# Reordering the pass over x in an induced-attention kernel: transposes, induced products, first chunk's scores and one projection

## The chip, the cores and the metric

One core of a Trainium2 chip runs the whole kernel. The metric is device time in microseconds (us) of one execution, lower is better; a kernel's figure is the median of several runs. Beside the runs there is one profiled execution, from whose trace every row below is taken. Engines: PE is the matmul engine (PEld its weight loads), DVE the vector engine, ACT the scalar engine, POOL the GpSimd engine, SP the engine that only issues DMAs here. A name such as SPq or ACTq is the engine's issuing side.

## What is computed

`x` has 12480 tokens of 128 features, `inducing` 32 rows of 128. Two attentions, then two MLPs of inner width 2048, all in float32 (the weights arrive as float64 and are narrowed on the chip):

```python
def mab(q, kv):
    s = scale * (q @ kv.transpose(0, 2, 1))
    s = s - s.max(-1, keepdims=True)
    a = np.exp(s)
    a /= a.sum(-1, keepdims=True) + 1e-09
    return a @ kv
h = mab(I, x)            # 32 inducing rows over all of x
y = mab(x, h)            # every token over the 32 rows of h
g = (y @ w_in1);  y1 = (g * np.cos(g)) @ w_out1
u = (y1 @ w_in2); y2 = (u / (1 + np.exp(-u))) @ w_out2
```

## The kernel before, in words

**Order.** Each engine runs its instructions in the order in which the program writes them (a manual schedule). Where an instruction waits, everything behind it on that engine waits too, and so it is on SP's queue of DMAs.

**Pass over x (the prologue).** The 98 token tiles are loaded in 8 heads, `heads = [(0, 8), (88, 10), (8, 16), (24, 16), (40, 16), (56, 16), (72, 11), (83, 5)]` (first tile, count), each in two halves, all from SP (L328, L330). Between heads 2 to 5 and their successors SP also issues four 512 KB pieces of the float64 weights (`fetch`, L133). Before the data come, PE does `SPIN` warm-up matmuls on zeros (L343). For each head k: PE transposes its tiles into PSUM (`transposes`, L392), ACT copies them out (`untile`, L402), PE forms the scores against the inducing rows (`scores`, L419), DVE takes their maximum (`maximum`, L432), PE and DVE fold it over the four groups (`row_max`, `bias`, `bound`, L442 to L469), ACT takes the exponentials and a rescaling factor (`exps`, L484, L498), DVE transposes them and adds up the denominators (`turn`, L507, L514), PE multiplies them with x (`induced`, L539), and DVE rescales the running sum (`rescale`, L552). In the loop over i, `induced` and `rescale` run two heads behind; the last three heads follow after the loop. In the same stretch POOL and DVE narrow the first weight pieces (`narrow_body` L142, `narrow_tail` L149, `narrow_sign` L154, `narrow_join` L157 and L165).

**Hand-over.** One matmul gives h transposed (L638), DVE copies it to `hT4` (L646). The first MLP's input weights are projected through h (`project`, L653, four pieces of 512 columns; `project_hi` on ACT, L662, and `project_lo` on DVE, L665, make them into `hw[0..3]`), since y @ w_in1 is a @ (h @ w_in1). ACT squares all of the narrowed w_in1 (`win`, L640) for a bound that selects one of two cosine forms (`flag`).

**Second attention.** Tokens go in chunks: 8 tiles, five of 16, 10 tiles. For a chunk PE forms scores (`weigh_scores`, L211), DVE transposes them, then come maximum, subtraction, exponential, sum, division, transposing back and a split in a high and a low part (`weigh_take` to `weigh_split`, L233 to L255). The first chunk does all of it in the prologue. Attention weights then go into `stk[:, b % 2, :]`, the right-hand side of the first MLP's matmuls for block b. For block 0 (tiles 0 to 3) this is done by eight small matmuls and a copy on ACT (L697, L704); for every other block by `spread` (L296), DMAs from SP: one per group of tokens and per quarter of the stack. Block 1 (tiles 4 to 7) has four groups, so 16 DMAs of 16 KB; a block of a 16-tile chunk has one group, so 4 DMAs.

**Main loop.** A step s handles unit u = s of the first MLP: eight units to a block. `mlp1_in` (L761) is the first thing that PE does in a step, then the down products of an earlier unit (`mlp1_out`, L853, L843); ACT takes the cosine (L796), DVE multiplies (L800). Unit u's `mlp1_in` writes one of two PSUM buffers, so it waits until DVE has multiplied unit u-2. Narrowing of further weights is spread over the steps by tables (`bodied`, `tailed`, `signed`, `joined`); `narrow_sign` and `narrow_join` share one buffer, `sign`, that POOL reads last. From step 11 on the second MLP runs beside the first.

## Time and profile before

| | us |
|---|---|
| median of 3 runs (lowest to highest) | 967.62 (966.91 to 967.96) |
| the profiled execution | 967.38 |
| its span in the trace | 965.2 |

The span runs from the first to the last instruction recorded; 2.2 us of the execution lie outside it. In the rows, a line gives a start in us from the span's beginning, a duration in us, the engine and line, operation, out<-in by names, the shapes and a count, and in square brackets the idle time before it with what ended it.

### The profile page before, as it was taken

The page shows a single profiled execution, that of the slowest core. Times are in us where ns is not written, and L with a number is a line of the kernel's source. Part 1 is how long each engine was busy: PE and PEld are TensorE (multiplying, and loading weights), DVE is VectorE, ACT ScalarE, POOL GpSimd, SP SyncE. Part 2 cuts the span into 40 slices and gives each one's busy share as a digit, 9 for nine tenths or more (in the row PEclk, how much of TensorE's full clock was granted, in tenths as well). Part 3 has the DMA queues.
Part 4 walks back from the last instruction along what each step waited for, and adds up shares of the span by engine and source line. Part 5 has one row for each costly group of instructions (what it writes and reads, how often), then busy time and mean ns, then how long its engine had stood idle before and what let it go on. Part 6 is the DMA issues. An engine that isn't in the chain of part 4 may idle for free.

```text
span 965.2 us, 11951 instructions
## 1 busy us (share of the span) xinstructions
PE 951.8 (99%) x4480; PEld 758.0 (79%) x4481; DVE 779.3 (81%) x784; ACT 691.6 (72%) x725; POOL 517.2 (54%) x274
## 2 busy tenths in 40 slices
PE   8899999999999999999999999999999999999997
PEld 5456778888878888878888887888887888888896
DVE  4889888988887988888988887988888888878751
ACT  5687768777668776767777777777767777677774
POOL 3346545654545655554655544655455554555565
PEclk9999999999999999999999999999999999999999
DMA  9341000001010010010010010010010100100001
GB/s 356 112 138 45 6 18 11 14 20 22 2 22 12 12 22 12 12 22 12 12 22 12 12 22 12 12 22 7 17 22 1 22 14 9 21 12 5 13 11 20
DMA packets 65484, 28.19 MB, mean 29 GB/s; under 512 B 54440, under 2 KB 60040, under 8 KB 65416
## 3 DMA queue, kind: packets, MB, share of 16 engines
q1 hardware_dynamic: 64760, 27.24, 10.8%
q8 instruction: 37, 0.61, 0.3%
q14 instruction: 31, 0.25, 0.1%
q10 hardware_dynamic: 656, 0.09, 0.1%
HBM read 14.79 MB, written 6.39 MB: 22 GB/s over the span
## 4 chain that ended last, share of the span: by engine, by line
PE 95%; DMA 2%; DVE 1%; issue 0%; SPq 0%; ACT 0%; POOL 0%; ACTq 0%; POOLq 0%; DVEq 0%
PE acc L843 53%; PE h L896 28%; PE h L761 9%; PE acc L853 4%; DMA x_sb<-in_x_dram 2%; PE s L211 1%; PE pt L392 0%; PE hp L539 0%; SPq L328 0%; PE s L419 0%; DVE et L507 0%; DVE c L800 0%; DVE mx L432 0%; POOL lo L925 0%; PE misc L455 0%
## 5 line engine op out<-in xcount | busy, mean ns | idle before, releaser
L920 POOL TENSOR_TENSOR lo<-s,hi 128x1024 fp32r<-128x1024 f32 (+3 forms) x189 | 446.7, 2364 | 381.0 <-ACT hi L919 359.6
L843 PE MATMUL acc<-hi,wo 128*128 128x512 f32 (+3 forms) x1520 | 406.8, 389 | 0.0
L843 PEld LDWEIGHTS acc<-hi,wo 128*128 128x128 f32 x1520 | 282.5, 188 | 61.5 <-issue 3.7
L800 DVE TENSOR_TENSOR h<-h,c 128x1024 f32<-128x1024 f32 (+3 forms) x188 | 226.1, 1203 | 123.9 <-ACT c L796 123.7
L796 ACT ACTIVATE c<-h,half_pi 128x1024 f32<-128x1024 f32 (+3 forms) x200 | 219.2, 1096 | 146.9 <-PE h L761 146.1
L911 ACT ACTIVATE s<-h 128x1024 f32<-128x1024 f32 (+3 forms) x200 | 201.2, 1006 | 76.6 <-PE h L896 71.8
L896 PE MATMUL h<-yhi,wi 128*128 128x512 f32 (+3 forms) x800 | 244.2, 386 | 0.0
L843 PE MATMUL acc<-lo,wo 128*128 128x512 f32 (+3 forms) x760 | 232.6, 387 | 0.1
L807 DVE CAST hi<-h 128x1024 fp32r<-128x1024 f32 (+3 forms) x188 | 224.9, 1196 | 6.5
L833 DVE TENSOR_TENSOR lo<-h,hi 128x1024 fp32r<-128x1024 f32 (+3 forms) x188 | 223.9, 1191 | 5.7
L919 ACT CAST hi<-s 128x1024 fp32r<-128x1024 f32 (+3 forms) x189 | 195.3, 1033 | 6.1
L896 PEld LDWEIGHTS h<-yhi,wi 128*128 128x128 f32 x800 | 148.8, 188 | 30.7 <-issue 0.5
L843 PEld LDWEIGHTS acc<-lo,wo 128*128 128x128 f32 x760 | 141.9, 188 | 31.2 <-POOL lo L925 0.4
L896 PE MATMUL h<-ylo,wi 128*128 128x512 f32 (+3 forms) x400 | 154.3, 386 | 0.0
L761 PE MATMUL h<-stk,hw 128*128 128x512 f32 (+3 forms) x400 | 126.0, 396 | 1.4 <-ACT stk L704 0.7
L761 PEld LDWEIGHTS h<-stk,hw 128*128 128x128 f32 x400 | 74.1, 188 | 26.8 <-issue 6.5
L896 PEld LDWEIGHTS h<-ylo,wi 128*128 128x128 f32 x400 | 75.1, 188 | 15.2
L877 ACT CAST yhi<-acc 128x512 fp32r<-128x512 f32 (+3 forms) x25 | 14.4, 576 | 15.1 <-PE acc L843 15.0
L943 DVE STREAM_TRANSPOSE o<-acc 128x512 f32<-128x512 f32 (+3 forms) x25 | 17.3, 694 | 9.3 <-PE acc L843 9.3
L853 PE MATMUL acc<-c,wf 128*128 128x512 f32 x48 | 22.5, 591 | 0.0
L878 DVE TENSOR_TENSOR ylo<-acc,yhi 128x512 fp32r<-128x512 f32 (+3 forms) x25 | 16.7, 669 | 5.4 <-ACT yhi L877 5.3
L800 DVE TENSOR_TENSOR c<-h,c 128x1024 f32<-128x1024 f32 x12 | 14.6, 1216 | 2.4 <-ACT c L796 1.9
(133 smaller groups left out, 320.6 us busy)
## 6 DMA issues: line engine op xcount, KB each, us to landing
out_dram<-o SPq DMA_DIRECT2D x80, 64.0 KB, 1.9
x_sb<-in_x_dram SPq DMA_DIRECT2D x8, 512.0 KB, 9.2
raw<-in_moe_w_in_dram SPq DMA_DIRECT2D x8, 512.0 KB, 6.5
raw<-in_moe_w_out_dram SPq DMA_DIRECT2D x8, 512.0 KB, 4.5
stk<-ahi SPq DMA_DIRECT2D x40, 64.0 KB, 2.0
stk<-at SPq DMA_DIRECT2D x40, 64.0 KB, 2.0
x_sb<-in_x_dram SPq DMA_DIRECT2D x3, 256.0 KB, 3.7
x_sb<-in_x_dram SPq DMA_DIRECT2D x2, 320.0 KB
```

What stands on the lines that cost most here:

```text
L761: nc.tensor.matmul(ps[:, a, 0:n], lhsT=hw[f // 4][:, f % 4 * P : (f % 4 + 1) * P], rhs=stacks[b][:, 0:n], start=True, stop=True,)
L796: nc.scalar.activation(cs, h, AF.Sin, bias=half_pi, scale=1.0)
L800: nc.vector.tensor_tensor(cs if whole else h, h, cs, ALU.mult)
L807: nc.vector.tensor_copy(hi[:, :, 0:n], h)
L833: nc.vector.tensor_tensor(lo[:, :, 0:n], h, hi[:, :, 0:n].bitcast(F32), ALU.subtract)
L843: nc.tensor.matmul(acc[:, 0:n], lhsT=wt[:, 2 * j + a, :], rhs=gt[:, a, 0:n], start=(j == 0 and p == 0 and a == 0), stop=(j == NJ - 1 and p ...
L853: nc.tensor.matmul(acc[:, 0:n], lhsT=w[:, 2 * j + a, :], rhs=c[:, a, 0:n], start=(j == 0 and a == 0), stop=(j == NJ - 1 and a == 1),)
L896: nc.tensor.matmul(ps[:, a, 0:n], lhsT=wt[:, fs], rhs=yt[:, 0:n], start=(p == 0), stop=(p == 2),)
L911: nc.scalar.activation(sv, hid2.pop(u)[:, :, 0:n], AF.Silu)
L919: nc.scalar.copy(hv, sv)
L920: nc.gpsimd.tensor_tensor(lv, sv, hv.bitcast(F32), ALU.subtract)
L943: nc.vector.transpose(o.rearrange("p t d -> p (t d)")[:, 0:n], acc2.pop(b)[:, 0:n])
```

## The change

- `SPIN` goes from 8 to 5, and the weight pieces are fetched after heads 3 to 6 instead of 2 to 5.
- `transposes(1, 0)` moves ahead of `scores(0)`. Head 0's transposed tiles lie tile by tile in `xF`, so ACT's copy is straight and `scores(0)` reads them with a stride.
- The loop does the induced products of heads 0 to 3 at i = 2, 3, 5, 6; those of heads 4 to 7 follow after the loop.
- Adding up the denominators moves from DVE (in `turn`) to POOL (`add_up`, after `exps`), and so does the small multiplication `foldz`.
- The narrowing of weight pieces 4 and 5 is scaled one place earlier and later in the program; the sign of piece 4 is taken just before `hT4` is written; the join of piece 5 goes from step 0 to step 1 of the main loop.
- The last piece of w_in1 lies in the buffer `s2`, `win` is a quarter shorter, and the squares are taken in two instructions.
- The first chunk's scores are formed token by token (the tile is the stationary operand, `hT4` the moving one), in two halves of four tiles. The first half is brought to the end in the prologue. The second half's maximum, subtraction and exponential are done there too; its division, transposing and split are left to steps 2, 4 and 5, and its 16 DMAs into `stk[:, 1, :]` are issued at the end of step 5.
- DVE instead of ACT copies block 0's stack; projection 3 with its two finishing instructions goes to step 1.

```diff
-    SPIN = 8
+    SPIN = 5
...
-            if 2 <= k < 2 + RAW:
+            if 3 <= k < 3 + RAW:
                 fetch()
...
+    rest = {
+        "span": (MT, FIRST - MT),
+        "s2": sft["at"][:, MT * Q : 2 * MT * Q].rearrange("p (t m) -> p t m", m=M),
+        "sm": sft["sm"][:, 0:MT, :],
+        "at": sft["at"][:, 0 : MT * Q],
+        "hi": sft["hi"][:, 0 : MT * Q],
+        "lo": sft["at"][:, 0 : MT * Q],
+    }
...
-    chunk_soft = [weigh_view(*span) for span in chunks]
+    chunk_soft = [rest] + [weigh_view(*span) for span in chunks[1:]]
...
+            if k == 0:
+                for g in range(G):
+                    nc.tensor.matmul(
+                        ps[g * Q : (g + 1) * Q, 0:WF],
+                        lhsT=indT,
+                        rhs=xF[:, :, g * Q : (g + 1) * Q],
...
+        def add_up(k):
             if k == 0:
-                nc.vector.tensor_copy(zacc[0], zk[:, 0:1])
+                nc.gpsimd.tensor_copy(zacc[0], zk[:, 0:1])
             else:
...
+                nc.gpsimd.tensor_scalar(
+                    zacc[k % 2],
+                    zacc[(k - 1) % 2],
+                    al[:, k : k + 1],
+                    zk[:, k : k + 1],
+                    ALU.mult,
+                    ALU.add,
+                )
...
+        transposes(1, 0)
         scores(0)
         maximum(0)
-        transposes(1, 0)
+        behind = {2: 0, 3: 1, 5: 2, 6: 3}
...
-            if 0 <= k < NP:
+            add_up(i - 1)
+            if 0 <= k <= NP:
                 narrow_body(k, True)
                 narrow_tail(k, True)
-            if i >= 2:
-                induced(i - 2)
+            if i in behind:
+                induced(behind[i])
...
+        h4, h5, h6, h7 = range(end - 3, end + 1)
         untile(end, 0)
         transposes(end, 1)
+        row_max(end - 1)
         untile(end, 1)
-        row_max(end - 1)
+        induced(h4, (0, KT // 2))
         scores(end)
...
+        induced(h4, (KT // 2, KT))
         row_max(end)
+        hps[h5] = other()
+        induced(h5, (0, KT // 2))
         turn(end - 1)
         bias(end)
         bound(end)
         exps(end)
...
+        add_up(end)
+        induced(h5, (KT // 2, KT))
+        rescale(h4)
+        induced(h6)
+        rescale(h5)
         turn(end)
-        narrow_sign(NP)
...
-        nc.vector.tensor_scalar_mul(foldz, fold, rz)
-        rescale(end)
+        nc.gpsimd.tensor_scalar(foldz, fold, rz, 1.0, ALU.mult, ALU.mult)
+        rescale(h7)
...
+        narrow_sign(NP)
         nc.vector.tensor_copy(hT4, misc[:C, None, 0:M].to_broadcast([C, G, M]))
...
+        half = [ps_s.tile([P, W], F32, tag="s1", name="s2") for _ in range(2)]
+        for t in range(FIRST):
+            nc.tensor.matmul(
+                half[t // MT][:, t % MT * M : (t % MT + 1) * M],
+                lhsT=xF[:, t, :],
+                rhs=hT4[:, 0, :],
...
+        for ps, e in zip(half, (eA[:, :, 0:M], eB)):
+            v = ps[:, 0 : MT * M].rearrange("p (t m) -> p t m", m=M)
+            nc.vector.tensor_reduce(out=mA, in_=v, axis=AX.X, op=ALU.max)
+            nc.vector.tensor_tensor(e, v, mA.to_broadcast(wide), ALU.subtract)
+            nc.scalar.activation(e, e, AF.Exp, scale=scale)
+        project(0)
...
+        nc.vector.tensor_reduce(out=mA, in_=eA, axis=AX.X, op=ALU.add)
+        nc.vector.reciprocal(mA, mA)
+        nc.vector.tensor_tensor(nA, eA[:, :, 0:M], mA.to_broadcast(wide), ALU.mult)
+        nc.vector.transpose(atA, flat(nA))
+        nc.scalar.copy(hiA, atA)
...
+        nc.vector.tensor_tensor(loA, atA, hiA.bitcast(F32), ALU.subtract)
         nc.scalar.activation(warm, ones, AF.Silu)
...
+        project_lo(hw[0], halves(0))
...
-        nc.scalar.copy(stk[:, 0, :], top)
+        project(2)
+        nc.vector.tensor_copy(stk[:, 0, :], top)
         stacks[0] = stk[:, 0, :]
-        spread(1, first | {"lo": lo0.bitcast(F32)})
...
+        for i in (1, 2):
+            project_hi(hw[i], halves(i))
+            project_lo(hw[i], halves(i))
...
-    joined = {5: 0, 6: 2, 7: 4, 8: 6, 9: 8, 10: 10, 11: 12, 12: 13, 13: 14, 14: 15, 15: 16}
+    joined = {5: 1, 6: 2, 7: 4, 8: 6, 9: 8, 10: 10, 11: 12, 12: 13, 13: 14, 14: 15, 15: 16}
...
+    rest_plan = {2: "norm", 4: "turn", 5: "split"}
...
-            for b in range(2, NB):
-                if s == b * NJ - (2 if b == 2 else 5 if blocks[b][0] == 1 else FILL):
+            for b in range(1, NB):
+                if s == b * NJ - (3 if b == 1 else 2 if b == 2 else 5 if blocks[b][0] == 1 else FILL):
                     spread(b, chunk_soft[blocks[b][0]])
...
             if s == 1:
-                soften(chunk_soft[1], "scores")
+                two = psh.tile([P, 2, 512], F32, tag="h2", name="s2")
+                nc.tensor.matmul(
+                    two[:, 0, :],
+                    lhsT=hT4.rearrange("c g m -> c (g m)"),
+                    rhs=flat(sft["s2"]),
...
+                weigh_scores(chunk_soft[1], two[:, 1, :])
...
+            if s == 1:
+                project_hi(hw[3], two[:, 0, :])
+                project_lo(hw[3], two[:, 0, :])
```

## Rows read from the trace of the kernel before

**Rows 1.** Busy us of each engine, share and instructions.

```profile
PE 951.8 (99%) x4480; PEld 758.0 (79%) x4481; DVE 779.3 (81%) x784; ACT 691.6 (72%) x725; POOL 517.2 (54%) x274
```

**Rows 2.** Busy time by stretch (count), then granted clock, DMA share, GB/s.

```profile
50.00:60.00 10.00, 10.00 (x29) 5.20 (x28) 9.04 (x13) 7.62 (x11) 3.59 (x4) 1.00 0.42 134
```

**Rows 3.** Timeline of the first 38 us: warm-up, transposes, products.

```profile
1.19 3.60 PE L343 MATMUL spin<-idle 128*128 128x512 bf16 x8 [1.19 <-DVE ones L351]
4.96 1.53 PE L392 MATMUL pt<-ident,x_sb 128*128 128x128 f32 x8
7.21 0.64 PE L419 MATMUL s<-xF,indT 128*32 128x256 f32 x8 [0.73 <-ACT xF L402]
21.05 1.06 PE L392 MATMUL pt<-ident,x_sb 128*128 128x128 f32 x8 [0.59 <-DMA x_sb<-in_x_dram]
22.13 1.06 PE L539 MATMUL hp<-x_sb,et 128*32 128x128 f32 x32
35.22 0.85 PE L539 MATMUL hp<-x_sb,et 128*32 128x128 f32 x22 [0.84 <-DVE hacc L552]
37.83 0.29 DVE L646 COPY hT<-misc 128x128 f32<-128x128 f32 x1 [0.50 <-PE misc L638]
```

**Rows 4.** Timeline from the first chunk's scores to the first unit.

```profile
39.90 0.52 DVE L238 TENSOR_TENSOR s<-s,m 128x256 f32<-128x256 f32 x1
43.58 0.62 PE L697 MATMUL st<-lo,pick 128*128 128x128 f32 x4
43.86 2.70 DVE L665 SCALAR_TENSOR_TENSOR hw<-hw,s_w,hwps 128x512 fp32r<-128x512 f32 x4
44.93 1.21 PE L761 MATMUL h<-stk,hw 128*128 128x512 f32 x4 [0.73 <-ACT stk L704]
```

**Rows 5.** DVE's timeline, units 0 to 2.

```profile
47.03 1.23 DVE L800 TENSOR_TENSOR c<-h,c 128x1024 f32<-128x1024 f32 x1 [0.48 <-issue]
48.18 0.42 DVE L154 TENSOR_SCALAR sign<-raw 128x512 int32<-128x512 int32 x1
48.63 0.69 DVE L157 SCALAR_TENSOR_TENSOR sign<-body,sign 128x512 int32<-128x512 int32 x1
49.24 1.22 DVE L800 TENSOR_TENSOR c<-h,c 128x1024 f32<-128x1024 f32 x1
50.77 0.43 DVE L154 TENSOR_SCALAR sign<-raw 128x512 int32<-128x512 int32 x1 [0.32 <-POOL wf L165]
51.12 1.22 DVE L800 TENSOR_TENSOR c<-h,c 128x1024 f32<-128x1024 f32 x1
```

**Rows 6.** Timeline of POOL's join and of the first MLP's units 2 and 8.

```profile
48.31 0.73 PE L761 MATMUL h<-stk,hw 128*128 128x512 f32 x2 [0.64 <-DVE c L800]
49.47 1.27 POOL L165 TENSOR_TENSOR wf<-sign,tail 128x512 int32<-128x512 int32 x1 [9.33 <-DVE sign L157]
61.09 1.02 PE L761 MATMUL h<-stk,hw 128*128 128x512 f32 x2
```

**Rows 7.** SP's timeline: block 1's spread, first and last of sixteen.

```profile
43.06 1.25 SPq L296 DMA_DIRECT2D stk<-ahi  x2
...
52.70 1.22 SPq L296 DMA_DIRECT2D stk<-lo  x2
```

**Rows 8.** Issuing time of these DMAs (ns, min/median/max); landing after issue.

```profile
L296 SPq DMA_DIRECT2D stk<-lo x8: 529/588/591, 44.4 to 53.3; - x8
DMA to landing us min/median/max: 1.7/1.8/3.3
```

**Rows 9.** Busy time by stretch at the kernel's end.

```profile
958.00:959.00 1.00, 0.48 (x2) 0.19 (x1) 0.35 (x1) 0.00 (x0) 0.16 (x1) 1.00 0.03 8
961.00:962.00 1.00, 0.00 (x0) 0.00 (x0) 0.00 (x0) 0.00 (x0) 0.00 (x0) 0.82 0.49 91
962.00:963.00 1.00, 0.00 (x0) 0.00 (x0) 0.00 (x0) 0.00 (x0) 0.00 (x0) 0.50 0.10 25
```

**Rows 10.** The chain of waits, the warm-up pair after the pass over x.

```profile
37.79 0.43 PE spin L343 x2
```

More of the change, by code (lines that the diff above doesn't have):

```diff
@@ L172, in narrowed @@
         if name == "in1":
-            return win[:, j * PC : (j + 1) * PC]
+            return flat(sft["s2"]) if j == NP - 1 else win[:, j * PC : (j + 1) * PC]
         if name in whole_of:
@@ L255, in weigh_split, with project_hi, project_lo @@
         lo_on.tensor_tensor(st["at"], st["at"], st["hi"].bitcast(F32), ALU.subtract)
+    rest = {
[6 more added lines that the diff above has]
+    }
+    def project_hi(h, ps):
+        nc.scalar.copy(h, ps)
+    def project_lo(h, ps):
+        nc.vector.scalar_tensor_tensor(
+            out=h,
+            in0=h.bitcast(F32),
+            scalar=s_w,
+            in1=ps,
+            op0=ALU.mult,
+            op1=ALU.add,
+        )
     blocks, first_of = [], []
@@ L602, in tile_induced_attention_then_two_mlps @@
         exps(end - 1)
-        narrow_body(NP, True)
-        narrow_tail(NP, True)
-        induced(end - 2, (0, KT // 2))
+        add_up(end - 1)
+        narrow_body(NP + 1, True)
+        narrow_tail(NP + 1, True)
+        induced(h4, (KT // 2, KT))
         row_max(end)
-        induced(end - 2, (KT // 2, KT))
+        hps[h5] = other()
+        induced(h5, (0, KT // 2))
         turn(end - 1)
@@ L626, in tile_induced_attention_then_two_mlps @@
         )
-        induced(end)
-        rescale(end - 1)
+        hps[h7] = other()
+        induced(h7)
+        rescale(h6)
         spin = ps_h.tile([P, SW], F32, tag="hp", name="spin")
@@ L659, in project @@
             )
-        def project_hi(i):
-            nc.scalar.copy(hw[i], hwps[i // 2][:, i % 2, :])
-        def project_lo(i):
-            nc.vector.scalar_tensor_tensor(
-                out=hw[i],
-                in0=hw[i].bitcast(F32),
-                scalar=s_w,
-                in1=hwps[i // 2][:, i % 2, :],
-                op0=ALU.mult,
-                op1=ALU.add,
-            )
-        first = chunk_soft[0]
-        weigh_scores(first, ps_s.tile([P, W], F32, tag="s1", name="s2")[:, 0:WF])
@@ L676, in tile_induced_attention_then_two_mlps @@
-        for i in range(3):
-            project(i)
-        sums = misc[0:1, 128 : 128 + M + 1]
-        nc.tensor.matmul(sums, lhsT=ones, rhs=sq, start=True, stop=True)
-        project(3)
-        weigh_take(first)
-        weigh_centre(first, nc.vector)
-        weigh_exp(first)
-        project_hi(0)
-        nc.scalar.activation(warm, ones, AF.Silu)
-        weigh_norm(first, nc.vector)
-        weigh_turn(first)
-        for i in range(1, 4):
-            project_hi(i)
-        hi0, at0 = first["hi"], first["at"]
@@ new lines, in tile_induced_attention_then_two_mlps @@
+        wide = [P, MT, M]
+        eB = rest["s2"]
+        for ps, e in zip(half, (eA[:, :, 0:M], eB)):
[4 more added lines that the diff above has]
+        project(0)
+        sums = misc[0:1, 128 : 128 + M + 1]
+        nc.tensor.matmul(sums, lhsT=ones, rhs=sq[:, 0 : M + 1], start=True, stop=False)
@@ new lines, in tile_induced_attention_then_two_mlps @@
+        nc.tensor.matmul(
+            sums[:, M : M + 1], lhsT=ones, rhs=sq[:, M + 1 : M + 2], start=False, stop=True
+        )
+        project(1)
+        project_hi(hw[0], halves(0))
+        nc.vector.tensor_reduce(out=mA, in_=eA, axis=AX.X, op=ALU.add)
[3 more added lines that the diff above has]
+        nc.scalar.copy(hiA, atA)
+        most = pw.tile([1, 2], F32, tag="top", name="most")
@@ L694, in tile_induced_attention_then_two_mlps @@
+        nc.vector.tensor_reduce(out=most[:, 0:1], in_=sums[:, 0:M], axis=AX.X, op=ALU.max)
+        nc.vector.tensor_tensor(most[:, 1:2], most[:, 0:1], sums[:, M : M + 1], ALU.mult)
+        nc.vector.tensor_scalar(flag, most[:, 1:2], 1.5**2, None, ALU.is_gt)
+        nc.vector.tensor_tensor(loA, atA, hiA.bitcast(F32), ALU.subtract)
+        nc.scalar.activation(warm, ones, AF.Silu)
+        project_lo(hw[0], halves(0))
         top = ps_s.tile([P, W], F32, tag="s1", name="st")
-        for i, v in enumerate((hi0, lo0)):
+        for i, v in enumerate((hiA, loA)):
@@ L992, in chunk_step @@
         def chunk_step(k, s):
+            if k == 0:
+                return rest_plan.get(s)
             if k == 1:
@@ L997, in attend @@
         def attend(s, early):
-            for k in range(1, NK):
+            for k in range(NK):
                 for at in (s, s + 0.25, s + 0.5):
```

83 lines of the change are left out of this document (45 added, 38 removed).

## The prediction

> **What bounds the kernel now.** I read the page first, for the engines' shares: PE is busy for 951.8 of 965.2 us [rows 1]. Then the busy time by stretch, to see where that share comes from: PE fills its stretch completely from 50 us on while the granted clock is 1.00 [rows 2], and it goes on so to its last matmuls [rows 9]. So a change that touches the first 50 us and eight steps after them can act in two ways only: unit 2's matmuls, from which PE has no more gaps (48.31 us, [rows 6]), move; or a gap opens later in PE, which nothing can win back. I therefore read the timeline of the first 62 us engine by engine, carry each edit forward to the start of unit 8 (61.09 us, [rows 6]), and put its shift on the end. The sum is made against the profiled execution, 967.38 us, 0.24 below the median of the three runs.
>
> **First transposes.** Three warm-up matmuls fewer are 3 x 3.60/8 = 1.35 us [rows 3]. They were over just before the first transposes, which showed no wait for their data, so the gain is between 0 (the tiles land no sooner) and 1.35; I take 0.4. Head 1's transposes fill the 0.73 us in which PE waited for ACT before the first scores [rows 3]; taken as 0.6. The strided reading of `xF` I cost at nothing: the same columns pass through PE. Together -1.0 us. Against it: the first eight warm-ups run at 0.45 us each, the pair after the pass at 0.215 [rows 3, 10], so PE begins at the lower of its two clock levels (1.2 of 2.4 GHz), whatever the stretch's 1.00 says. With less work ahead of the transposes it may stay there longer; at 0 to 1.5 us, I put it at 0 and keep the rest for the range.
>
> **The loop.** PE waited 0.59 us for head 5's tiles [rows 3]; now one 512 KB piece fewer stands ahead of them on SP's queue, and the wait goes. A head's induced products take up to 1.06 us of PE [rows 3]; they leave the loop at i = 4 and come back behind it. There PE has waits to put them in (0.84 us ahead of one group alone, [rows 3]). I take -1.2 us for the loop and +0.1 for the stretch behind it; bounds -0.6 (the wait alone) and -1.8. The denominators' sums on POOL are small beside its scalings and only the last one is near the path. The sign of piece 4 now fills DVE's 0.50 us of idle time before `hT4` [rows 3] and leaves the path of the last heads; with `foldz` now passing through POOL I count the two as equal.
>
> **From hT4 to the first unit.** Before: hT4 ends at 37.83 + 0.29 = 38.12, unit 0 starts at 44.93, 6.81 us [rows 3, 4]. After, with DVE's price for 128x128 between the 0.29 of the copy and the 0.52 of a subtraction twice as wide [rows 3, 4], 0.32 taken: eight passes of 128-wide weights on PE, 8 x 0.13 [rows 3], 1.05; maximum and subtraction of both halves, 4 x 0.32; sum, reciprocal, product and transposing back, 1.15; three small flag operations, which cover ACT's copy, 0.5; low part 0.33; `project_lo` of piece 0, 2.70/4 = 0.68 [rows 4], which covers the four low matmuls (0.62, [rows 4]); DVE's copy of the stack 0.75, which with projection 2 on PE is 0.3 more than it was on ACT; gaps 0.1. That is 6.1, so -0.7 us. Bounds -1.2 and 0. The prologue thus gives -1.0 - 1.2 + 0.1 - 0.7 = **-2.8 us** at unit 2.
>
> **Steps 1 to 5: DVE.** From here I count from DVE's first product (47.03 us before, [rows 5]). Products, signs and joins follow each other at 1.15, 0.45 and 0.61 us from start to start [rows 5]. Before, the third product began at 51.12 - 47.03 = 4.1. Now step 1 has join 5 and directly behind it sign 6, which must wait until POOL has read `sign`: 0.84 us from the join's start to POOL's, and POOL's 1.27 [rows 5, 6]. Product 1 starts at 1.6, the join at 2.75, POOL ends at 4.85, sign 6 starts at 4.9, then comes the new `project_lo` of piece 3 (0.68), and product 2 starts at 5.9, 1.8 later than before. Unit 4 waits for its buffer; PE's pitch is (61.09 - 48.31)/6 = 2.13 us [rows 6], so it cannot catch up. Step 2 adds the second half's sum, increment and reciprocal on DVE, about 0.8 us: another 0.35 at unit 5. PE would be ready for unit 8 at 16.2 instead of 61.09 - 47.03 = 14.1: **+2.2 us** if nothing else held it. Bounds 0 (cosines or PE were later anyway) and 2.6.
>
> **Step 8: the spread.** Before, SP issued block 1's sixteen DMAs from 43.06 to 53.92 [rows 7], over 7 us ahead of unit 8, so they cost nothing. Now they come behind step 5. DVE transposes the second half in step 4, at 12.3 to 12.6 by the count above; ACT's high part is ready at 12.9, POOL's low part, behind join 7, at 14.2. Two DMAs go at once, fourteen after that. One takes SP 0.529 to 0.588 us [rows 8], and the last two of sixteen started 9.64 us after the first two [rows 7]; at 0.63 from start to start the last starts at 14.3 + 13 x 0.63 = 22.5 and lands 1.8 later [rows 8], at 24.3. `mlp1_in` of unit 8 is PE's first work in step 8 and reads the whole stack, so unit 8 and everything behind it on PE waits from 16.2 to 24.4: 8.1 us. Unit 8 thus moves from 14.1 to 24.4, **+10.3 us** including the 2.2 above. Without DVE's delay it is +8.1. While PE stands, DVE, ACT and POOL finish step 7 and can go no further.
>
> The Trainium skill's page "DMA: Bandwidth & Descriptors", section "Issuing engines are not separate DMA queues", says that the time which a sequencer takes to initiate a DMA "is usually small relative to the DMA itself". The trace disagrees here, 0.59 us against 1.8 from issue to landing [rows 8]; by the rule the spread would be in place about 2 us after the low part, at 16.3, and the time would be that of the hidden spread below.
>
> **The clock after the gap.** At the kernel's end PE's last matmuls are at 958.5; the granted clock falls at about 961.6 and is 0.50 from 962 on [rows 9]. A gap of 8.1 us is longer than that, so I expect the lower level when unit 8 starts. At the kernel's start the warm-ups stayed there for all of their 3.60 us [rows 3, 10]; as much again would lose half of it, **+1.7 us**. Bounds 0 and 3.
>
> **Sum.** 967.38 - 2.8 + 10.3 + 1.7 = 976.6 us.
>
> **Rivals.** *Cheaper gap* (chance 0.2): the wait is there, but the clock stays up (974.9), or DVE's delay is hidden and the clock stays up (967.38 - 2.8 + 8.1 = 972.7). For it: the lower level never shows in the middle of this trace; against it, there is no comparable gap. *No gain ahead* (0.12): the pass over x does not get shorter, because loads set its pace or PE's clock rises later; then 976.6 + 2.1 = 978.7. For it speaks the wait for x [rows 3]. *Hidden spread* (0.1): the transfers are in place when unit 8 comes. Then 967.38 - 2.8 + 2.2 = 966.8, or 964.6 if DVE's delay is hidden too: faster or the same. It needs 14.3 + 13d + 1.8 - 14.1 - 2.8 below 0, an issue pitch d under 0.06 us; the lowest in the trace is 0.529 [rows 8]. *Forecast* (0.58): 976.6.
>
> **How the numbers follow.** I forecast the likeliest, 976.6. The range takes in the cheaper gap and the missing gain, and leaves out the hidden spread and the far ends: 971.8 (972.7 with 0.9 more won in the prologue) to 979.6 (978.7 with 0.9 more lost to the clock). A difference of under 0.2%, 1.9 us, cannot be told from none here. Slower holds all cases but the hidden spread, 0.9; of that, same 0.04 and faster 0.06, since an error in the reading of the queue would bring the gain of the prologue with it.
>
> **What would show it.** Unit 0 at about 42.1 us and DVE's first product near 44.2; DVE idle for some 1.4 us behind join 5, waiting for POOL; sixteen DMAs of 16 KB on SP from about 57 to 67 us; PE idle some 8 us at the first matmul of unit 8, released by a DMA into `stk`; a stretch with granted clock below 1.00 behind it. A spread issued before step 4, a pitch far under 0.5 us, or PE without a gap between 55 and 70 us would make the prediction wrong.

## The result, and the profile after

| | before | after |
|---|---|---|
| median (lowest to highest), us | 967.54 (966.91 to 967.96) | 980.22 (979.06 to 981.21) |
| runs | 4 | 4 |
| the profiled execution, us | 967.38 | 980.07 |
| its span, us | 965.2 | 978.3 |

The changed kernel takes 1.013 times as long, 95% interval 1.0117 to 1.0143: 12.7 us slower. That is the forecast's sign, and 0.6 us above the upper end of its range.

I read the rows of after in the order of the prediction's steps: up to unit 2, unit 2 to unit 8, behind unit 8. First PE's timeline up to unit 2 (to be set beside [rows 3, 4, 6]).

```profile
1.19 2.32 PE L365 MATMUL spin<-idle 128*128 128x512 bf16 x5 [1.19 <-DVE ones L373]
...
3.68 1.97 PE L421 MATMUL pt<-ident,x_sb 128*128 128x128 f32 x8
6.66 0.74 PE L421 MATMUL pt<-ident,x_sb 128*128 128x128 f32 x5 [1.01 <-DMA x_sb<-in_x_dram]
7.33 0.64 PE L447 MATMUL s<-xF,indT 128*32 128x256 f32 x8
...
9.84 0.71 PE L462 MATMUL s<-xT,indT 128*32 128x320 f32 x8
...
29.27 0.78 PE L462 MATMUL s<-xT,indT 128*32 128x352 f32 x8
...
31.15 0.27 PE L484 MATMUL misc<-ident,mx 128*1 128x128 f32 x1 [0.74 <-DVE mx L474]
...
36.02 0.38 PE L675 MATMUL misc<-zacc,fold 128*128 128x1 f32 x2 [0.69 <-POOL zacc L558]
...
37.56 0.38 PE L694 MATMUL misc<-foldz,hacc 128*128 128x32 f32 x2
...
43.41 0.66 PE L761 MATMUL st<-hiA,pick 128*128 128x128 f32 x4 [0.87 <-ACT hiA L750]
...
45.39 1.17 PE L823 MATMUL h<-stk,hw 128*128 128x512 f32 x4
...
49.03 0.72 PE L823 MATMUL h<-stk,hw 128*128 128x512 f32 x2 [0.62 <-DVE c L862]
```

The same marks in the kernel before: the scores of head 1 (`128x320`, ten tiles), those of head 6 (`128x352`, eleven tiles), and the product that ends the pass.

```profile
10.44 0.71 PE L419 MATMUL s<-xT,indT 128*32 128x320 f32 x8
...
30.53 0.78 PE L419 MATMUL s<-xT,indT 128*32 128x352 f32 x8
...
37.38 0.41 PE L638 MATMUL misc<-foldz,hacc 128*128 128x32 f32 x2
```

Unit 0 starts at 45.39 us instead of 44.93, unit 2 at 49.03 instead of 48.31. Where the forecast has 2.8 us won, 0.7 are lost. The first transposes start 1.28 us earlier, but head 1's, now in front of the scores, wait 1.01 us for their data. Head 1's scores still come 0.60 us sooner than before and head 6's 1.26 sooner; behind these the lead is lost, and the pass ends 0.18 us later.

Then PE around unit 8, and SP's queue in the same stretch (to be set beside [rows 6, 7]).

```profile
61.50 0.98 PE L823 MATMUL h<-stk,hw 128*128 128x512 f32 x2
62.32 1.88 PE L915 MATMUL acc<-c,wf 128*128 128x512 f32 x4
72.32 1.19 PE L823 MATMUL h<-stk,hw 128*128 128x512 f32 x2 [8.12 <-DMA stk<-at]
73.31 3.62 PE L915 MATMUL acc<-c,wf 128*128 128x512 f32 x4
75.94 1.72 PE L823 MATMUL h<-stk,hw 128*128 128x512 f32 x2
```

```profile
60.70 1.25 SPq L318 DMA_DIRECT2D stk<-ahi  x2
...
69.58 1.22 SPq L318 DMA_DIRECT2D stk<-at  x2
```

PE stands for 8.12 us, and what ends it is a DMA into the stack: the sixteen were issued from 60.70 to 70.80 us. From unit 2 to unit 8 it takes 72.32 - 49.03 = 23.29 us, before 61.09 - 48.31 = 12.78 [rows 6]: +10.51. The first four `acc` matmuls behind the gap take 3.62 us instead of the 1.88 ahead of it. The busy time by stretch tells why; columns: the stretch, its length, busy us (and instructions) of PE, PEld, DVE, ACT and POOL, then the granted clock, DMA share and GB/s.

```profile
64.00:66.00 2.00, 0.20 (x1) 0.00 (x0) 1.76 (x3) 0.27 (x2) 1.26 (x1) 1.00 0.11 26
66.00:68.00 2.00, 0.00 (x0) 0.00 (x0) 0.36 (x1) 0.55 (x1) 1.26 (x1) 0.78 0.10 25
68.00:70.00 2.00, 0.00 (x0) 0.00 (x0) 0.00 (x0) 0.00 (x0) 0.00 (x0) 0.50 0.10 25
...
74.00:76.00 2.00, 2.00 (x5) 0.81 (x3) 1.30 (x2) 1.22 (x2) 0.00 (x0) 0.50 0.79 313
76.00:78.00 2.00, 2.00 (x6) 1.11 (x5) 0.52 (x1) 0.31 (x1) 1.28 (x1) 0.66 0.00 0
78.00:80.00 2.00, 2.00 (x7) 1.06 (x6) 1.16 (x2) 1.97 (x4) 0.00 (x0) 1.00 0.00 0
```

PE's last matmul ahead of the gap ends at 64.20; the clock goes to 0.50 (1.2 GHz) in the stretch from 66 to 68 and is at 1.00 (2.4 GHz) again from 78. DVE, ACT and POOL do nothing from 68 to 72. From unit 8 to the end of the span it takes 978.3 - 72.32 = 905.98 us, before 965.2 - 61.09 = 904.11: +1.87. So the span's +13.1 us are 0.72 + 10.51 + 1.87; the execution is 12.7 us longer, since 0.4 us less of it lie outside the span.

DVE's timeline of units 0 to 2 shows the wait that the prediction had behind join 5 (to be set beside [rows 5]).

```profile
50.41 0.68 DVE L157 SCALAR_TENSOR_TENSOR sign<-body,sign 128x512 int32<-128x512 int32 x1
52.55 0.43 DVE L154 TENSOR_SCALAR sign<-raw 128x512 int32<-128x512 int32 x1 [1.46 <-POOL wf L165]
52.89 0.74 DVE L271 SCALAR_TENSOR_TENSOR hw<-hw,s_w,s 128x512 fp32r<-128x512 f32 x1
53.55 1.22 DVE L862 TENSOR_TENSOR c<-h,c 128x1024 f32<-128x1024 f32 x1
```

### The profile page after: what moved, and what is told of

It is laid out like the page before. It is cut to its first block, busy times and chain, and to the rows that moved or that the text cites. A ratio compares the mean times of both kernels' runs of the same rounds, so it can differ in the third digit from the quotient of the medians.

```text
span 978.3 us, 11983 instructions
## 1 busy us (share of the span) xinstructions
PE 955.7 (98%) x4488; PEld 760.3 (78%) x4488; DVE 778.4 (80%) x779; ACT 692.3 (71%) x729; POOL 521.4 (53%) x286
## 3 DMA queue, kind: packets, MB, share of 16 engines
HBM read 14.79 MB, written 6.39 MB: 22 GB/s over the span
## 4 chain that ended last, share of the span: by engine, by line
PE 94%; POOL 1%; DVE 1%; SPq 1%; ACT 1%; issue 1%; DMA 1%; ACTq 0%; POOLq 0%; DVEq 0%
PE acc L905 52%; PE h L958 27%; PE h L823 9%; PE acc L915 3%; SPq L318 1%; PE pt L421 1%; DMA x_sb<-in_x_dram 0%; PE s L211 0%; POOL wf L165 0%; DVE sign L157 0%; PE hwps L711 0%; ACT e L526 0%; POOL win L165 0%; POOL body L142 0%; DVE sign L154 0%
```

## The experiments

All ratios are to runs of the kernel before on the same chip (its median there was 967.2 to 967.6 us). Three questions: is the gap SP's queue and what does the clock cost; why is unit 2 not earlier; does a mended version beat both kernels.

### The gap at unit 8

**e_half.** Only two of block 1's four groups are spread: eight DMAs instead of sixteen. The other half of the stack is set to zero once at the start, so block 1 is computed from part of its weights.

```diff
-        for g, t, m, at, n in places(b):
+        for g, t, m, at, n in places(b)[:groups]:
...
```

> Leaves out 8 of block 1's 16 DMAs (that half of the stack is zero, so block 1's tokens of two groups are wrong). Theory (SP issues one DMA every 0.63 us and the last issue sets unit 8): PE's wait of 8.12 us at unit 8 falls by 8 x 0.63 = 5.1 to about 3.1, and since that gap is short the granted clock stays at 1.00, which gives back about 1.9 more: 980.2 - 5.1 - 1.9 = 973.2 us. Rival (a late low part, or the landing of the transfers, sets the wait, not their number): the wait stays near 8 us and the time near 980.

Measured: 975.12 us (972.84 to 976.1), 1.008 times before (1.0063 to 1.0097). The profiled execution took 972.84, the lowest of the four, and shows a wait of 3.09 us:

```profile
67.67 0.71 PE L824 MATMUL h<-stk,hw 128*128 128x512 f32 x2 [3.09 <-DMA stk<-at]
68.21 1.88 PE L916 MATMUL acc<-c,wf 128*128 128x512 f32 x4
```

The wait goes with the number of DMAs: 5.03 us less for eight fewer, 0.63 each. In this execution the clock stayed up (1.88 for four `acc`). The other three runs were 2 to 3 us longer. They have no trace, but their mean granted clock is 0.995 to 0.996 instead of 0.998, so PE was at its lower level for some time in them; how much of the 2 to 3 us that is stays open.

**e_late.** The kernel before, with block 1's spread at the end of step 5, all of its data ready since the prologue. The low part lies in another buffer, where it stays that long; nothing else is changed.

```diff
-        spread(1, first | {"lo": lo0.bitcast(F32)})
+        first["lo"] = lo0.bitcast(F32)
...
-            for b in range(2, NB):
-                if s == b * NJ - (2 if b == 2 else ...):
+            for b in range(1, NB):
+                if s == b * NJ - (3 if b == 1 else 2 if b == 2 else ...):
```

> The kernel before with one part of the change alone: the spread of block 1 (the same sixteen DMAs, all data ready since the pass) issued at the end of step 5 instead of ahead of the main loop. Theory (SP's queue is served in order, 0.63 us each): SP starts them behind step 4's weight fetch near 55 us, the last lands near 66.7, unit 8 waits about 5.6 us from 61.09, and the clock behind it costs up to 1.9: median 973.1 to 975.0. Rival (the transfers are hidden anyway, and the wait in the changed kernel comes from its late data, not from the place of the spread): unit 8 at 61.1, median 967.5.

Measured: 974.88 us (973.89 to 976.58), ratio 1.0079 (1.0064 to 1.0095). SP's timeline and PE's:

```profile
54.66 10.11 SPq L296 DMA_DIRECT2D stk<-ahi  x16
```

```profile
59.19 1.88 PE L853 MATMUL acc<-c,wf 128*128 128x512 f32 x4
66.30 1.19 PE L761 MATMUL h<-stk,hw 128*128 128x512 f32 x2 [5.23 <-DMA stk<-ahi]
67.29 3.60 PE L853 MATMUL acc<-c,wf 128*128 128x512 f32 x4
```

So the place of the spread alone makes most of the loss, 7.6 us of it: sixteen DMAs one behind the other, 10.11/16 = 0.63 us each, although all of their data were ready. Here too the clock is at the lower level behind the gap.

**e_warm.** The changed kernel, with 32 matmuls into an unused bank in the gap, from data already there.

```diff
+            if s == NJ:
+                gap = psh.tile([P, 2, 512], F32, tag="h2", name="gap")
+                for _ in range(32):
+                    nc.tensor.matmul(gap[:, 0, :], lhsT=hw[0][:, 0:P], rhs=stacks[0], ...)
```

> Adds 32 matmuls (7 us of PE at 2.4 GHz) into an unused PSUM tile ahead of unit 8, inside the wait; unit 8 still comes with the last DMA at about 72.3 us. Theory (1.9 us are lost behind unit 8 because the clock fell in the gap): the granted clock stays at 1.00 through the gap and behind it, and the time falls by 1.9 to 978.3 us. Rival (the 1.9 us come from weight pieces that were fetched late, behind the spread on SP): no change, 980.2.

Measured: 978.25 us (977.74 to 980.13), 1.0113 (1.0096 to 1.013); in the profile unit 8 is at 72.37, the clock is 1.00 throughout, and unit 8 to the end takes 976.6 - 72.37 = 904.23 us. That is 0.12 above the 904.11 of before, so nearly all of the 1.87 us behind unit 8 are the clock's.

**e_early.** The second half's sum, increment, division, transposing and split go to step 0, its DMAs to the end of step 1.

```diff
-    rest_plan = {2: "norm", 4: "turn", 5: "split"}
+    rest_plan = {0: "norm", 0.25: "turn", 0.5: "split"}
...
-                if s == b * NJ - (3 if b == 1 else ...):
+                if s == b * NJ - (7 if b == 1 else ...):
```

> The second half's division, transposing and split move from steps 2, 4 and 5 to step 0, and the 16 DMAs are issued at the end of step 1. Theory: the spread ends at about 62.5 us, ahead of unit 8, so the wait (8.1) and the clock's loss (1.9) go; DVE's work is the same, only earlier: 980.2 - 10.0 = 970.2 us, still 2.7 above the kernel before. Rival (the spread is only the last of several late things, for instance the narrowed weights of the next steps): PE finds another wait near unit 8 and the time stays above 975.

Measured: 973.81 us (973.16 to 974.68), 1.0063 (1.0046 to 1.008). Unit 8 (67.60) waits for nothing, and the clock is 1.00. But 3.6 us more are left than I expected: units 3 and 4 now wait for DVE's products; on ACT the copy of the high part is queued ahead of a cosine that one of them needs. In this execution unit 0 was also late already, at 46.85 instead of 45.39, by the pass over x.

```profile
54.92 0.74 PE L823 MATMUL h<-stk,hw 128*128 128x512 f32 x2 [1.99 <-DVE c L862]
...
59.18 0.73 PE L823 MATMUL h<-stk,hw 128*128 128x512 f32 x2 [1.81 <-DVE c L862]
```

**e_join0.** The join of piece 5 back in step 0: `joined = {5: 0, ...}`.

> Join 5 goes back from step 1 to step 0. Theory (in step 1 DVE waits 1.46 us for POOL between join 5 and sign 6, and this delay is carried to unit 8 and into the spread): that wait falls to about 0.3, unit 4 no longer waits 1.18 us for DVE, the split and the spread come about 1.2 us earlier: 979.0 us, with PE's wait at unit 8 still near 8 us. Rival (DVE's delay is covered, since the spread alone sets unit 8): no change, 980.2.

Measured: 980.88 us (980.39 to 981.49), 1.0137 (1.012 to 1.0154), no better than after. Unit 4's wait went and unit 0 to unit 8 got 1.03 us shorter (25.90 instead of 26.93), but this execution started unit 0 at 46.21, 0.8 later, and took 906.79 us behind unit 8. A gain of a microsecond here is as large as what two executions differ by, so its size at the end is open; that it doesn't remove the gap (8.15 us) is shown.

### Why unit 2 is not earlier

**e_spin8.** The changed kernel with `SPIN = 8`.

> Eight warm-up matmuls again instead of five; all else as changed. Theory (the three that were taken away left PE at its lower clock through the first transposes, and head 1's tiles land at 5.7 to 7.0 us whatever PE does): the first eight transposes take about 1.5 us instead of 1.97, head 1's transposes still start with the landing, and the time is the same or up to 0.7 us lower: 979.5 to 980.2. Rival (fewer warm-ups do bring the pass forward): the time rises by about 1 us to 981.2.

Measured: 980.51 us (980.33 to 981.75), 1.0137 (1.0121 to 1.0152). The first transposes start at 4.96 instead of 3.68 and the first scores at 7.44 instead of 7.33. So taking away three warm-ups (1.35 us) brought 0.1 us in these two executions, and the time shows no gain either. One pair of profiles can't price it more closely: in the eight profiles with five warm-ups and head 1's transposes in front (after, e_warm, e_half, e_hifirst, e_join0, e_early, e_adddve, e_addlate) the first scores start between 6.39 and 8.08, half of them before 7.22; in the five with the order of before (before, e_late, e_fetch, e_loop, e_prod) between 6.72 and 7.25, the middle one at 7.21.

**e_hifirst.** ACT's copy of the first half's high part ahead of `project_hi` of piece 0 on ACT's queue.

```diff
-        project_hi(hw[0], halves(0))
...
         nc.scalar.copy(hiA, atA)
+        project_hi(hw[0], halves(0))
```

> ACT copies the high part of the first half ahead of the first piece of the projection instead of behind it. Theory (the projection's copy waits for PE's second projection and holds the high part for 0.7 us): unit 0 comes 0.65 us sooner after hT4, 979.6 us. Rival (PE's third projection, which stands ahead of unit 0, sets it): under 0.2 us.

Measured: 979.6 us (979.13 to 981.3), 1.0128 (1.0113 to 1.0144). From the product that ends the pass to unit 0 it took 45.19 - 38.06 = 7.13 us, in after 45.39 - 37.56 = 7.83: the 0.87 us wait for `hiA` is gone. The three mended versions below have this edit too and take 7.15 to 7.16, so the 0.7 us are no accident of one execution. In after ACT's `project_hi` waits for a projection on PE until 42.57, and the copy stands behind it.

**e_addlate.** On POOL the sums are queued behind the scalings, and the last scalings behind the last sum.

```diff
-            add_up(i - 1)
             if 0 <= k <= NP:
                 narrow_body(k, True)
                 narrow_tail(k, True)
+            add_up(i - 1)
...
```

> The denominators' sums stay on POOL but stand behind the two scalings of a weight piece instead of ahead of them. Theory (each sum waits for ACT's rescaling factor and holds the scalings, the join and so DVE's next sign behind it: DVE waited 0.99 and 0.48 us for POOL, PE 0.69 us for the last sum): these waits go and the matmul that ends the pass (37.56 us) comes about 1.2 us earlier, 979.0 us. Rival (PE's or DVE's own work fills the pass by then): under 0.3 us.

Measured: 981.71 us (981.42 to 983.24), 1.0151 (1.0137 to 1.0165). Missed: the product that ends the pass is at 38.92. The loss is in the loop, where the sums were to get out of the way: head 6's scores come 21.24 us behind head 1's, in after 19.43. PE waits 0.83 us there for tiles of x, as it does in some executions of after's pass too (below). The rest is new: DVE still waits 0.99 us for POOL's join, the two narrowing instructions behind it take 0.94 and 1.02 us beside POOL's scalings (0.44 and 0.73 in after), and PE stands 1.67 us for DVE's next maximum (0.87 in after).

```profile
26.36 0.94 DVE L154 TENSOR_SCALAR sign<-raw 128x512 int32<-128x512 int32 x1 [0.99 <-POOL win L165]
27.34 1.02 DVE L157 SCALAR_TENSOR_TENSOR sign<-body,sign 128x512 int32<-128x512 int32 x1
```

Behind head 6's scores it takes 7.90 us, 0.39 less than in after, although the last scalings now stand ahead of `foldz`:

```profile
37.63 0.65 POOL L149 TENSOR_SCALAR tail<-raw 128x512 int32<-128x512 uint32 x1
38.38 0.49 POOL L691 TENSOR_SCALAR foldz<-fold,rz 128x32 f32<-128x32 f32 x1
```

**e_adddve.** Sums and `foldz` back on DVE, at their places of before.

```diff
-                nc.gpsimd.tensor_scalar(zacc[k % 2], zacc[(k - 1) % 2], al[:, k : k + 1], ...)
+                nc.vector.scalar_tensor_tensor(out=zacc[k % 2], in0=zacc[(k - 1) % 2], ...)
```

> The changed kernel with the sums of the denominators and foldz back on DVE. Theory (POOL's queue gave back what the loop had won): DVE's waits for POOL ahead of the signs (0.99 and 0.48 us) go, and with them the last sum's wait and foldz on POOL (0.69 and 0.29); the matmul that ends the pass starts near 36.1 us instead of 37.56, unit 0 near 43.9 instead of 45.39, the spread and unit 8 move along, median about 978.7. Rival (the loop's pace is set elsewhere, by PE or the tiles' landing): the matmul moves by less than 0.3 us, median 980.2.

Measured: 981.11 us (980.61 to 982.45), 1.0142 (1.0127 to 1.0158); the product that ends the pass is at 37.65. The expected 1.5 us didn't come, but the place did show: from head 6's scores to that product it takes 7.36 us, in after 8.29, so 0.93 is got back where POOL's last sum and `foldz` had stood. But the loop ahead of it took 20.26 us instead of 19.43, with no wait for tiles in either. In its second half DVE's sums now take 0.58 to 0.79 us each; in e_prod, below, 0.18 to 0.23. So POOL's queue gave back what was won, and with the sums on DVE the loop gives it back instead.

**e_loop, e_prod, e_fetch.** The kernel before with parts of the change alone. e_loop has the later fetch, the induced products of heads 0 to 3 at i = 2, 3, 5, 6 with the changed order behind the loop, and the sign of piece 4 just before `hT4` (`et` gets a third buffer, as in after). e_prod is e_loop without the later fetch; e_fetch is the later fetch alone. Sums stay on DVE. Below, the first hunk stands in e_loop and e_fetch, the second in e_loop and e_prod.

```diff
-            if 2 <= k < 2 + RAW:
+            if 3 <= k < 3 + RAW:
...
-            if i >= 2:
-                induced(i - 2)
+            if i in behind:
+                induced(behind[i])
...
```

> The kernel before with one part of the change alone: weight pieces fetched one head later, induced products three heads behind at i = 2, 3, 5 and 6 with the changed order behind the loop, the sign of piece 4 just before hT4; sums stay on DVE, warm-up at 8, first chunk, joins and spread as before. Theory: the pass is shorter by 1.0 to 1.9 us (hT4 copy at 36.0 to 36.8 instead of 37.83), median about 966.1. Rival (what the loop wins is given back behind it whatever POOL does, since the same products stand there instead): hT4 within 0.4 us of before, median 967.5.

> As e_loop, but the weight pieces are fetched as before, so only the induced products, rescalings and the sign of piece 4 stand elsewhere. Theory (DVE sets the loop's pace, not PE; what e_loop won was given back because the later pieces put POOL's scalings beside DVE's instructions with two inputs, zacc 0.89 instead of 0.18 us and sign<-body 1.16 instead of 0.69): these two are back at 0.2 and 0.7 us, and the matmul that ends the pass starts 0.3 to 0.9 us before the 37.38 of the kernel before, median 967.0. Rival (the products come back behind the loop and cost there what they won): 37.2 to 37.7, median 967.5.

> The kernel before with the fetch of the weight pieces one head later and nothing else. Theory: PE's wait of 0.59 us for head 5's tiles goes, but zacc and sign<-body take 0.5 to 1.6 us more in all beside POOL's scalings, so the pass ends 0 to 0.9 us later than 37.38, median 967.9. Rival (the wait for tiles was the limit): it ends 0.6 earlier, median 966.9.

Measured: e_loop 967.64 us (967.22 to 969.47), ratio 1.0004 (0.9995 to 1.0013); e_prod 967.23 (966.56 to 968.82), 0.9999 (0.999 to 1.0008); e_fetch 967.11 (966.45 to 968.35), 1.0 (0.9991 to 1.0009). None differs from before, alone or together. The profiles say where the pieces went. The table has the start of the first scores, and the time from there to the scores of head 1, on to those of head 6 (and how much of it PE waited for tiles of x), on to the product that ends the pass, and on to unit 0, in us:

| kernel | first scores at | to head 1's | to head 6's (waits for tiles) | to the last product | to unit 0 |
|---|---|---|---|---|---|
| before | 7.21 | 3.23 | 20.09 (0.59) | 6.85 | 7.55 |
| e_late (pass as before) | 7.21 | 3.22 | 19.49 (0) | 6.85 | 7.55 |
| e_fetch | 6.72 | 3.22 | 20.33 (0) | 6.85 | 7.54 |
| e_loop | 6.82 | 3.23 | 20.02 (0) | 7.50 | 7.55 |
| e_prod | 7.25 | 3.23 | 19.50 (0.28) | 7.50 | 7.55 |
| after | 7.33 | 2.51 | 19.43 (0) | 8.29 | 7.83 |
| e_warm (pass as after) | 7.11 | 2.84 | 19.36 (0) | 8.27 | 7.83 |
| e_early (pass as after) | 8.08 | 3.35 | 19.30 (0) | 8.29 | 7.83 |
| e_join0 (pass as after) | 7.70 | 2.51 | 19.87 (0.35) | 8.30 | 7.83 |
| e_half (pass as after) | 6.39 | 2.51 | 20.75 (1.04) | 8.28 | 7.83 |
| e_hifirst (pass as after) | 7.00 | 2.51 | 20.25 (0.69) | 8.30 | 7.13 |
| e_adddve | 7.43 | 2.60 | 20.26 (0) | 7.36 | 7.87 |
| e_mend2 | 6.74 | 2.52 | 20.64 (0.56) | 7.33 | 7.15 |
| e_mend3 | 7.46 | 2.51 | 20.33 (0) | 7.37 | 7.15 |

The last two columns hardly differ between executions of the same code, so they can be read to a tenth. Behind head 6's scores the products that were moved out of the loop cost 0.65 us (7.50 instead of 6.85), and the sums and `foldz` on POOL another 0.8 to 0.9 (8.29, against 7.50 and 7.36). The column to head 1's scores has the gain of the new order of transposes, 0.7 us in most profiles.

The loop, up to head 6's scores, differs between executions of one code by as much as PE waits there for tiles: before took 20.09 with a wait of 0.59 [rows 3], e_late, with the very same pass, 19.49 with none. Without these waits it takes 19.5 in before's pass and 19.3 to 19.7 in after's, so nothing that can be told apart was won. The later fetch did not do away with the waits either: three of the six executions of after's pass have them, up to 1.04 us. So what I had forecast as won there was a wait of one execution. And where the later fetch meets sums on DVE (e_fetch, e_loop, e_adddve, e_mend2), the loop takes 20.0 to 20.3 without the waits; e_mend3, with the fetch of before, is no shorter, so the fetch is not all of it.

The busy time by stretch tells why the loop doesn't follow PE. This is the loop's second half in e_prod, and then in e_loop.

```profile
22.00:33.00 11.00, 10.10 (x187) 6.08 (x184) 9.46 (x25) 6.82 (x15) 6.06 (x7) 1.00 0.82 268
```

```profile
22.00:33.00 11.00, 9.24 (x175) 5.98 (x171) 9.84 (x24) 6.59 (x15) 7.88 (x9) 1.00 0.81 267
```

Both engines are busy for most of the stretch, and each waits for the other in it (PE for the maximum, DVE for its fold). Where PE is freer, in e_loop, DVE is the busier one, 9.84 of 11 us, with one instruction fewer than in e_prod. DVE's rows and POOL's in e_fetch show how:

```profile
20.01 1.04 DVE L514 SCALAR_TENSOR_TENSOR zacc<-zacc,al,zk 128x1 f32<-128x1 f32 x1
...
22.16 1.22 DVE L157 SCALAR_TENSOR_TENSOR sign<-body,sign 128x512 int32<-128x512 int32 x1
```

```profile
19.77 1.27 POOL L165 TENSOR_TENSOR win<-sign,tail 128x512 int32<-128x512 int32 x1
22.13 0.69 POOL L142 TENSOR_SCALAR body<-raw 128x512 f32<-128x512 f32 x1 [1.09 <-DMA raw<-in_moe_w_in_dram]
22.91 1.01 POOL L149 TENSOR_SCALAR tail<-raw 128x512 int32<-128x512 uint32 x1
```

In e_prod the same two instructions of DVE, with POOL in other places, took:

```profile
20.77 0.18 DVE L514 SCALAR_TENSOR_TENSOR zacc<-zacc,al,zk 128x1 f32<-128x1 f32 x1
...
22.73 0.69 DVE L157 SCALAR_TENSOR_TENSOR sign<-body,sign 128x512 int32<-128x512 int32 x1
```

**e_prodx.** e_prod with head 1's first transposes ahead of the first scores.

> As e_prod, with head 1's first transposes ahead of the first scores as well (layouts unchanged). Theory: PE's 0.73 us of waiting for ACT before the first scores are filled, and maximum and all behind it come 0.3 to 0.5 us sooner than in e_prod where head 1's tiles land in time, median 966.6. Rival (those tiles land at 5.7 to 7.0 us, so PE waits for them instead and the scores come later): as e_prod or up to 0.4 slower.

Measured: 967.82 us (966.52 to 968.38), 1.0002 (0.9993 to 1.0011). In the profile head 1's scores come 2.59 us behind the first ones (e_prod 3.23), but the first ones came later, at 7.62: the thirteen transposes ahead of them took 2.74 us, 0.21 each where e_fetch's eight took 1.09, 0.14 each, so PE was still at its lower level for part of them. Further on PE waited 0.89 and 0.66 us for x, and nothing of the gain was left at the end of the pass (38.37). That the tiles of x take the gain back is argued from this one profile; the median shows no gain.

### A mended version

**e_mend.** The changed kernel with e_hifirst, e_addlate, e_join0 and `SPIN = 8`; the second half is brought to its end on DVE right ahead of product 0, split on POOL, and its DMAs go at the end of step 0.

```diff
+        weigh_norm(rest, nc.vector)
+        weigh_turn(rest)
+        weigh_split(rest, nc.gpsimd.tensor_copy, nc.gpsimd)
...
-    rest_plan = {2: "norm", 4: "turn", 5: "split"}
+    rest_plan = {}
```

> All mends at once: second half finished in DVE's gap before the first product and split on POOL, its 16 DMAs issued at step 0, join 5 in step 0, sums behind the scalings, the high part first, eight warm-ups. Theory (the four places named are the whole loss): the gap (8.1), the clock (1.9), DVE's delay in steps 1 to 5 (2.4, of which 0.7 stays for the last piece of the projection) and 1.9 of the prologue go: 980.2 - 8.1 - 1.9 - 1.7 - 1.9 = 966.6 us, about 1 below the kernel before. Rival (token-major scores and the later induced products cost something of their own): 968 or more.

Measured: 970.84 us (970.06 to 971.92), 1.0035 (1.0022 to 1.0049). No gap at unit 8 (64.17); what is left stands ahead of it. The pass ends at 38.76, with the losses of e_addlate: again PE stood 1.66 us in the loop for a maximum of DVE, the granted clock was 0.50 from 30 to 32 us, and `foldz` stands behind POOL's scalings. Unit 2 is at 51.09, 1.76 us of it waiting for product 0, which stands behind the new work.

**e_mend2.** As e_mend, with sums and `foldz` on DVE and the new work ahead of `project_lo` of pieces 1 and 2.

> The changed kernel with every loss found so far mended: sums and foldz on DVE, ACT's copy of the high part ahead of project_hi(0), join of piece 5 in step 0, 8 warm-ups, the second half brought to its end on DVE right behind the copy of block 0's stack (split on POOL) and its sixteen DMAs at the end of step 0. Theory: no gap at unit 8, clock 1.00 throughout, pass-ending matmul near 36.3, unit 0 near 43.6, the second half's chain costs unit 2 about 1.4 us, unit 2 near 48.6, median about 967.5, no better than before. If POOL's sums were not what held the last mend: unit 2 near 51, median 970.8. Faster than before by over 1 us (966.4 or less) only if the second half's chain hides behind PE's projections.

**e_mend3.** As e_mend2, with the weight pieces fetched as before.

> The mended kernel that equals the one before (e_mend2), with the weight pieces fetched as before. Theory: without the meeting of POOL and DVE in the loop the pass ends 0.5 to 0.9 us sooner (37.23 before that edit), unit 2 near 47.6, median 966.8. Rival (the fetch decides nothing): 967.5.

Measured: e_mend2 967.51 us (966.32 to 968.83), ratio 1.0001 (0.9992 to 1.001); e_mend3 967.65 (967.42 to 968.85), 1.0005 (0.9996 to 1.0014). In e_mend2 unit 2 stands at 48.31 and unit 8 at 61.10, both as in [rows 6]:

```profile
48.31 0.74 PE L826 MATMUL h<-stk,hw 128*128 128x512 f32 x2
...
61.10 1.02 PE L826 MATMUL h<-stk,hw 128*128 128x512 f32 x2
```

Halving the first chunk's scores is kept there, with its DMAs issued from 48.73 on, and all 12.7 us are back. e_mend3 missed its 0.5 to 0.9 us: its pass ends at 37.67, no sooner than e_mend2's (37.23), and the place of the fetch decides nothing that can be measured.

No version beat the kernel before, yet not because nothing was won. In e_mend2 and e_mend3 head 1's scores come 0.7 us sooner behind the first ones, and unit 0 comes 0.4 sooner behind the pass. Against that the moved products cost 0.5 behind head 6's scores, and from unit 0 to unit 2 it takes 3.93 us instead of 3.38. These four add up to about nothing. The second and the last may be one and the same: projection 3, 1.0 us of PE, went from ahead of unit 0 to behind it, where PE also waits 0.74 us (before 0.47) for DVE's `project_lo`, which now stands behind the second half's work. Whether the new order of transposes by itself is worth anything at the end was not run.

## Why the prediction failed

Mechanism, sign and size of the large terms were right. **The step that failed is the gain ahead of unit 2, "-1.0 - 1.2 + 0.1 - 0.7 = -2.8 us":** the trace has +0.72, a difference of 3.5. It was the rival *No gain ahead*, but its 978.7 priced the missing gain at 2.1, and the rest of the difference lifts the time above the range; its reasons, loads and a late clock, are the smaller part of what was found. By its terms, each read from one mark to the next as in the table:

- *First transposes, -1.0:* -0.60 at head 1's scores. The "0.6" for the new order came (2.51 us instead of 3.23 behind the first scores). The 0.4 for fewer warm-ups did not: the first scores are 0.12 us later, since head 1's transposes, now ahead of them, waited 1.01 us for tiles that landed at 6.6 us. I had read a wait on PE as free room without asking when the data of what I put there land.
- *The loop, -1.2:* -0.66 up to head 6's scores. Nearly all of it is the wait for head 5's tiles, 0.59, the lower bound of this term, and that is a matter of the execution (e_late). That it falls within the bounds is luck; the products' part is worth nothing here. I counted PE's time per head, where PE and DVE wait for each other in turn.
- *The stretch behind it, +0.1:* +1.44, the largest miss. The products that come back find less room than I took (0.65, e_loop and e_prod), and POOL's queue costs 0.8. "The denominators' sums on POOL are small beside its scalings" held for their length (0.34 us) and not for their place: the last stands behind POOL's scalings, and PE waits 0.69 us for it; PE also waits 0.74 for a maximum of DVE (0.28 in e_prod), which had waited 0.48 for POOL's join. "With `foldz` now passing through POOL I count the two as equal" is part of the same error. e_adddve gets 0.93 back in this stretch and loses 0.83 in the loop.
- *hT4 to unit 0, -0.7:* +0.31. ACT's queue was left out of it. `project_hi` waits for PE, and the copy of the high part behind it for both, so three flag operations (to 42.70) don't cover a copy that ends at 43.35. e_hifirst gets 0.70 back, and a gain of 0.4 is left. The terms of the list add up to 5.8 as they stand, and to 6.1 only if the copy's 0.3 is counted on top.
- Unit 0 to unit 2 took 3.64 us instead of 3.38, for which the forecast had nothing; the copy of `hT4`, against that, came 0.03 sooner behind its product.

The sum -0.60 - 0.66 + 1.44 + 0.31 + 0.26 - 0.03 is 0.72.

**The other terms held.** The wait of DVE behind join 5 was forecast as 1.4 us and is 1.46. Unit 2 to unit 8 was forecast as +10.3 and is +10.51, PE's idle time in it 8.1 and 8.12. The DMAs of "about 57 to 67 us" ran from 60.70 to 70.80, 3.7 us later, of which the missing gain is 3.5. e_half and e_late show the cause apart from everything else: SP's queue at 0.63 us for each DMA. So *Hidden spread* and *Cheaper gap* are out for this kernel; that the clock can stay up at a gap of 3.1 us is in e_half's profile.

The clock was forecast as +1.7 and is +1.87, and e_warm gets it back. That it would fall was right; that the size fits so well is in part luck. The forecast took 3.60 us at the lower level and half of them lost. The granted clock stayed low for some 5 us behind unit 8 (the stretches from 72 to 78), unit 11 starts at 80.99 instead of e_warm's 78.59, and some of these 2.4 us come back further on.

## What to carry to other kernels

A transfer of many small DMAs has a length of its own on its queue, count times issue pitch; it needs that much time between its last input and its reader, and moving it later by a few steps can cost more than all that the move was to win. Before you count a gain in a stretch where two engines wait for each other in turn, follow both, and follow the queue of every engine to which an instruction is moved: what stands ahead of it there, and for whom that waits. A wait seen in one execution, for a load above all, is not yet a wait to be won; look for it in a second trace of the same code, and read small gains only in stretches that come out alike in both.

## What the runs showed of the hardware

**DVE and POOL stop each other.** An instruction of DVE on 128x1 took 1.04 us instead of 0.18, and ended at 21.05, as POOL's join, begun at 19.77, did at 21.04 (e_fetch). `sign<-body` took 1.22 instead of 0.69 beside POOL's scaling, and the scaling behind it 1.01 instead of 0.66 to 0.68. The Trainium skill, page "SBUF — State Buffer", section "Who interferes with whom", says that a DVE instruction with two SBUF inputs contends with a GpSimd instruction that reads SBUF, that the port pair they share is an exclusive lock, and that the order of issue decides who blocks. The trace agrees in both directions. It would explain why a new place for POOL's work so often cost DVE what it won elsewhere, since each place meets other instructions of DVE. That is argued from these rows; no run took the meeting away by itself.

**The start of the kernel varies.** The eight transposes of head 0 took 1.09 us in e_fetch, 1.53 in before and 1.62 in e_prod, behind the same eight warm-ups, and 1.97 in after behind five. After's warm-ups took 0.46 us each, twice the 0.215 of [rows 10]. So PE is at its lower level first, for a time that differs between executions, although the granted clock reads 1.00 there. Head 1's tiles land at different times too: where PE waited for them, its transposes went on at 5.72 (e_half) to 7.03 us (e_join0). In six executions of after's pass (after, e_warm, e_half, e_hifirst, e_join0, e_early) the last product starts between 37.56 and 39.02, and after's is the earliest of them. That is why the pass is read by differences within a profile, and only where they repeat.
